# A linear-attention, gated-MLP and gated-convolution chain on one core: the left-over key block is padded to full height, the weight splits end in a one-pass sum, the list scheduler has other rules, and batch 2's attention is placed in batch 1

## The chip, the cores and the metric

The program runs on one core of one Trainium2 chip. A core has five engines that run their own instruction streams and wait for each other by semaphores: TensorE (PE, matmuls into PSUM), VectorE (DVE), ScalarE (ACT, activations and copies), GpSimd (POOL) and SyncE (SP, which here issues nearly all DMA transfers). The metric is the device time of one execution in microseconds (us), as the median over runs; lower is better.

## The reference, cut to what matters

Three blocks follow one another, with B = 8 batches, 8 heads of 64, 576 tokens, model width 512 and inner width 1024:

```python
# 1 attention without a score matrix (q, k, v: [8, 8, 576, 64])
q_s = softmax(q, over the 64 of a head);  k_s = softmax(k, over the 576 tokens)
x = q_s @ (k_s^T @ v)                      # heads are put side by side: [8, 576, 512]
# 2 spatially gated MLP
u, v = split(gelu_tanh(x @ w_in), 2)       # 512 wide each
v_n = layernorm(v) * g_ln
x2 = x + (u * (w_sg @ v_n + b_sg)) @ w_out
# 3 convolution gate
h = relu(x2 @ w_in2)                       # 1024 wide
c = depthwise_conv3(h, conv_w)             # along the tokens
out = (h * sigmoid(c)) @ w_out2
```

The weights arrive as 64-bit floats and have to be used at more than single-pass precision. So the kernel writes each operand as a high part and a low part, both in a 32-bit format that TensorE takes in one pass (`F32R`), and makes each product from three matmuls (hi·hi, hi·lo, lo·hi; `mm3`, L477).

## The kernel before

**Phases.** Phase 1 does blocks 1 and 2 for batches 0 to 7, phase 2 does block 3 for all batches. Block 2's result goes to a DRAM tensor `x2d` and is read back in phase 2. A batch of phase 1 is a list of 29 groups (L1186 on): four `hv` units (the v half of x @ w_in, 128 tokens each), eight `hu` units (the u half), eight `mx` units (w_sg times v_n), and eight `wo` units (times w_out). The function `insert(b, i)` (L1165) puts the attention of a later batch behind group `i` of batch `b`.

**Attention of a batch.** `attend_k` (from `k_steps`, L605) takes the maximum of the key tile `kt` over the tokens on DVE: maxima over column blocks (`top`), then transposes and swaps (`spread`), all in the scratch tiles `scr` and `r`; POOL subtracts it from `kt`, ACT takes the exponential. The keys lie as [128 tokens, 4 blocks of 512 columns], and the 64 tokens that are left over from 576 = 4·128 + 64 stand in a fifth, half-wide block of `kt`: its upper 64 partitions hold heads 0 to 3, its lower 64 the others. `attend_q` (`q_steps`, L665) does the softmax of the query tiles `q0` to `q3`, and the left-over query tile `q4` has its own seven steps (`left_max` to `left_tr` in `k_steps`, scratch `lm` and `lx`). `back_kv(b, c2)` (L707) multiplies the keys with the values `vt` for two of four pairs of heads; the ones column of `vt` gives the softmax sum, and DVE divides by it into `kvd`. For the left-over block its matmuls contract over 64 rows alone. It is called twice for a batch, and the second call issues the loads of the next batch's `kt` and `vt`. `xt` and `xt_left` multiply `kvd` with the queries.

**Weights.** `split` (L485) turns a 64-bit weight block into its two parts with bit operations on DVE and copies on ACT. For 12 blocks the low part is summed on TensorE (L522): `one`·a − hi + `one`·lf, where `one` is the identity matrix in F32; 32 further blocks of 256 columns (`split_far`) are summed on POOL and written to DRAM for phase 2.

**Order.** The code above issues nothing by itself. Each call is recorded, with a price (`price`, L220) and its dependences, and `Plan.order` (L285) simulates the engines: TensorE takes whole units (from `begin` to `begin`), the first one that would not stall among the next `WINDOW` = 8; the other engines take the ready instruction whose latest start is smallest. The sequence that comes out is what each engine's stream holds, so the recorded line of every instruction is L429, in `emit`. Two of the rules are touched: how long a DVE instruction and a POOL instruction that meet hold each other up (`start`, L327), and the choice of an instruction (L406 on).

Of the kernel before, what the change touches and what calls it, by code (L numbers as in the profile page):

```python
# [152 lines left out]
class Plan:  # L153
    WINDOW = 8
# [32 lines left out]
    def add(self, eng, name, args, kw):  # L187
        n = self.node(eng, name, args, kw)
        out = kw["out"] if "out" in kw else args[0]
        ins = [a for a in list(args[0 if "out" in kw else 1:]) + [v for k, v in kw.items() if k != "out"] if isinstance(a, View)]  # L190
        for v, w in [(a, False) for a in ins] + ([(out, True)] if isinstance(out, View) else []):
            self.touch(n, v, w)
        self.price(n, out, ins)
        return n
# [25 lines left out]
    def price(self, n, out, ins):  # L220
# [10 lines left out]
        elif e == "pe":  # L231
            m = size(out)
            if name == "transpose":
                n.cost = 0.22
            elif ins[0].tile.dtype == F32:
                n.cost = 0.09 if m == 65 else 0.71 if m == 512 else 0.19
            else:
                n.cost = max(0.111, 0.0045 + m * 0.000447)
            n.lat = n.cost + 0.17
        elif e == "act":  # L240
            n.cost = (0.155 if psum else 0.195) + cols * 0.00085
            if isinstance(n.kw.get("scale"), View) or isinstance(n.kw.get("bias"), View):
                n.cost += 0.05 + min(cols, 500) * 0.0001
            n.lat = n.cost + 0.07
            f = args_func(n)
            n.table = {"Gelu_apprx_tanh": "g", "Exp": "e", "Sigmoid": "s"}.get(f)
        elif e == "pool":
# [3 lines left out]
            if "tensor" in name:  # L251
                wide = any(o[0] == "to_broadcast" for v in views for o in v.ops)
                n.cost = 0.95 if cols == 1 else 0.2 + cols * (0.0008 if name == "tensor_copy" else 0.00164 if wide else 0.0021)
# [3 lines left out]
            n.shared = True  # L257
        else:
            two = sum(v.tile.space != "psum" for v in ins) > 1 and not psum and name in ("tensor_tensor", "scalar_tensor_tensor")
# [5 lines left out]
            n.shared = (two or fast) and cols > 60  # L265
# [19 lines left out]
    def order(self):  # L285
# [20 lines left out]
        poolend = [0.0]  # L306
        vecend = [0.0]
# [19 lines left out]
        def start(n, t):  # L327
# [3 lines left out]
            if n.eng == "dve" and n.shared and poolend[0] > t:  # L331
                more = min(cost, poolend[0] - t) * 1.0
                cost, lat = cost + more, lat + more
            if n.eng == "pool":
                if vecend[0] > t:
                    more = min(0.5, vecend[0] - t)
                    cost, lat = cost + more, lat + more
                poolend[0] = t + cost
            if n.eng == "dve" and n.shared:
                vecend[0] = t + cost  # L340
# [32 lines left out]
        while events:  # L373
# [4 lines left out]
            while again:  # L378
                again = False
                for k in self.real:  # L380
# [30 lines left out]
                    if can:  # L411
                        key = lambda n: (n.late + (2.0 if n.table and n.table != table[0] else 0.0), n.i)
                        n = min(can, key=key)
                        queue[k].remove(n)
                        start(n, t)
                        again = True
# [3 lines left out]
        return out  # L420

# [16 lines left out]
def attn_gated_conv_kernel(ctx, tc, q, k, v, q0, k0, w_in, g_ln, w_sgT, b_sg, w_out, w_in2, conv_w, w_out2, out):  # L438
# [46 lines left out]
    def split(slot, src, hi, lo, n, modes, stores=(), behind=None):  # L485
# [11 lines left out]
        lf, hf = l.bitcast(F32), h.bitcast(F32)  # L497
# [10 lines left out]
        dve.tensor_scalar(h, a.bitcast(U32), 0xFF800000, None, ALU.bitwise_and)  # L508
        (pool if hi is not None else dve).tensor_tensor(lf, lf, hf, ALU.mult)
        if hi is None:  # L510
            dve.tensor_tensor(lo, a, lf, ALU.add)
            return
        if modes is None:
# [6 lines left out]
            pe.matmul(ps, one, lf, start=False, stop=True)  # L520
            act.activation(lo, ps, AF.Copy)
            return  # L522
        modes[0].tensor_tensor(a, a, r32(hi), ALU.subtract)
        modes[1].tensor_tensor(lo, a, lf, ALU.add)
        for t, d in zip((hi, lo), stores):
            sp.dma_start(d, r32(t))
# [45 lines left out]
    vt = at.tile([128, 18, 2, 65], F32, name="vt")  # L572
    qt = {b: [None] * 5 for b in range(B)}
# [5 lines left out]
    def q_tile(b, c):  # L579
        qt[b][c] = at.tile([128, 512 if c < 4 else 256], F32, tag=f"q{c}", name=f"q{c}", bufs=2)  # L580
        return qt[b][c]

    def load_q(b):
        for c in range(4):
            sp.dma_start(q_tile(b, c), q[b, :, c * 512:c * 512 + 512])

    def load_left(b):
        sp.dma_start(q_tile(b, 4), q[b, :, 2048:2304])

    def load_v(b):  # L590
        sp.dma_start(vt[:, :, :, 0:64], v[b])
# [13 lines left out]
    def k_steps(b):  # L605
# [29 lines left out]
        def ex():  # L635
            act.activation(kt, kt, AF.Exp)

        qv = qt[b][4].rearrange("p (j a) -> p j a", a=32)
        lm = at.tile([128, 8], F32, tag="lm", name="lm")
        lx = at.tile([128, 8], F32, tag="lx", name="lx")  # L640

        def left_max():
            dve.tensor_reduce(lm, qv, axis=AX.X, op=ALU.max)
            swap32(lx, lm, CFG['sl'][min(b - 1, 2)])
            dve.tensor_tensor(lm, lm, lx, ALU.max)
            pool.tensor_tensor(qv, qv, lm.unsqueeze(2).to_broadcast([128, 8, 32]), ALU.subtract)

        def left_exp():
            act.activation(qv, qv, AF.Exp)
            dve.tensor_reduce(lm, qv, axis=AX.X, op=ALU.add)  # L650

        def left_mul():
            swap32(lx, lm, CFG['sl'][min(b - 1, 2)])
            dve.scalar_tensor_tensor(lm, lm, 1e-9, lx, ALU.add, ALU.add)
# [917 lines left out]
```

## Time and profile before

| | us |
|---|---|
| median of 3 runs | 951.65 |
| lowest and highest run | 951.44 and 953.36 |
| span of the profiled execution | 952.6 |
| TensorE busy, VectorE busy | 926.2, 772.9 |
| ScalarE busy, GpSimd busy | 543.7, 317.8 |

The profiled execution is told by its span, from its first instruction to its last; nothing that lies around the span is listed for it. Its span lies between the lowest and the highest run, 0.95 us above the median. A matmul's recorded duration is a modelled one and overlaps the next matmul's; how fast TensorE goes is read from the distance between two starts. Almost all rows carry L429, so groups are told apart by the names of their tiles: `mm` and `acc` are PSUM tiles, `wsl` the staging tile of the weight blocks for phase 2, `wAh` and `wAl` the parts of w_in. An F32 matmul has two records in the trace, an F32R matmul one.

### The profile page before, as it was taken

The page shows a single profiled execution, that of the slowest core. Times are in us where ns is not written, and L with a number is a line of the kernel's source. Part 1 is how long each engine was busy: PE and PEld are TensorE (multiplying, and loading weights), DVE is VectorE, ACT ScalarE, POOL GpSimd, SP SyncE. Part 2 cuts the span into 40 slices and gives each one's busy share as a digit, 9 for nine tenths or more (in the row PEclk, how much of TensorE's full clock was granted, in tenths as well). Part 3 has the DMA queues.
Part 4 walks back from the last instruction along what each step waited for, and adds up shares of the span by engine and source line. Part 5 has one row for each costly group of instructions (what it writes and reads, how often), then busy time and mean ns, then how long its engine had stood idle before and what let it go on. Part 6 is the DMA issues. An engine that isn't in the chain of part 4 may idle for free.

```text
span 952.6 us, 16062 instructions
## 1 busy us (share of the span) xinstructions
PE 926.2 (97%) x6026; PEld 821.1 (86%) x6026; DVE 772.9 (81%) x1477; ACT 543.7 (57%) x1113; POOL 317.8 (33%) x334
## 2 busy tenths in 40 slices
PE   5999999999999999999999999999999999999997
PEld 4578877988988889889899999998989888988895
DVE  7978989888888879889876348998798969886773
ACT  6776454655746645635643335544767656675663
POOL 6335454555636635737634000201120202020000
PEclk9999999999999999999999999999999999999999
DMA  9741614172482653812548572001111111121011
GB/s 316 194 147 32 175 65 116 43 201 69 119 208 78 193 133 94 215 59 90 122 138 256 154 218 71 34 12 70 37 50 45 73 34 51 45 73 34 7 39 56
DMA packets 54663, 99.17 MB, mean 104 GB/s; under 512 B 5332, under 2 KB 29012, under 8 KB 52792
## 3 DMA queue, kind: packets, MB, share of 16 engines
q1 hardware_dynamic: 50888, 89.88, 30.1%
q0 software_dynamic: 3696, 8.26, 5.0%
q8 instruction: 47, 0.77, 0.3%
q14 instruction: 32, 0.26, 0.1%
HBM read 62.59 MB, written 35.53 MB: 103 GB/s over the span
## 4 chain that ended last, share of the span: by engine, by line
PE 85%; DVE 9%; DMA 2%; ACT 2%; issue 1%; POOL 0%; SPq 0%; ACTq 0%
PE mm L429 57%; PE acc L429 28%; DVE wsl L429 2%; DVE sm L429 1%; DMA wsl<-in_w_in 1%; DVE scr L429 1%; DMA wsl<-in_w_out 1%; DVE r L429 1%; DVE vnl L429 1%; DVE xl L429 1%; DVE gl L429 1%; DMA sgh<-in_q 1%; DVE lm L429 0%; DVE u L429 0%; DVE x2s L429 0%
## 5 line engine op out<-in xcount | busy, mean ns | idle before, releaser
L429 DVE SCALAR_TENSOR_TENSOR cv<-h,cw,cv 128x576 f32<-128x576 f32 x128 | 111.9, 875 | 17.3 <-ACT cv L429 15.5
L429 PE MATMUL acc<-wAh,yl 128*128 128x512 f32 x256 | 101.8, 397 | 0.0
L429 PE MATMUL acc<-wAh,yh 128*128 128x512 f32 x256 | 100.8, 394 | 0.7 <-ACT yh L429 0.7
L429 PE MATMUL acc<-wAl,yh 128*128 128x512 f32 x256 | 101.0, 395 | 0.0
L429 PE MATMUL mm<-sgh,vnh 128*128 128x288 f32 x256 | 81.4, 318 | 1.5 <-DVE u L429 1.0
L429 PE MATMUL mm<-xh,w2h 128*128 128x288 f32 x280 | 82.8, 296 | 0.0
L429 PE MATMUL mm<-xh,w2l 128*128 128x288 f32 x280 | 82.4, 294 | 0.0
L429 PE MATMUL mm<-xl,w2h 128*128 128x288 f32 x280 | 82.4, 294 | 0.0
L429 PE MATMUL mm<-xh,wAh 128*128 128x288 f32 x256 | 79.3, 310 | 2.9 <-DVE xl L429 1.4
L429 PE MATMUL acc<-gh,wouth 128*128 128x288 f32 x256 | 81.2, 317 | 0.0
L429 PE MATMUL acc<-gl,wouth 128*128 128x288 f32 x256 | 76.3, 298 | 1.1 <-DVE gl L429 1.0
L429 PE MATMUL mm<-sgh,vnl 128*128 128x288 f32 x256 | 75.5, 295 | 0.6 <-DVE vnl L429 0.6
L429 PE MATMUL acc<-gh,woutl 128*128 128x288 f32 x256 | 75.8, 296 | 0.0
L429 PE MATMUL mm<-xh,wAl 128*128 128x288 f32 x256 | 75.5, 295 | 0.0
L429 PE MATMUL mm<-xl,wAh 128*128 128x288 f32 x256 | 75.5, 295 | 0.0
L429 PE MATMUL mm<-sgl,vnh 128*128 128x288 f32 x256 | 75.4, 294 | 0.0
L429 ACT ACTIVATE cv<-cv 128x576 f32<-128x576 f32 x64 | 43.7, 683 | 54.7 <-DVE cv L429 54.7
L429 POOL TENSOR_TENSOR wsl<-wsl 128x256 f32<-128x256 f32 (+1 forms) x66 | 50.7, 768 | 60.5 <-DVE wsl L429 23.7
L429 POOL TENSOR_TENSOR q<-q,qm 128x512 f32<-128x512 f32 x56 | 61.5, 1123 | 20.5 <-DVE qm L429 18.9
L429 POOL TENSOR_TENSOR kt<-kt,scr 128x512 f32<-128x512 f32 (+1 forms) x42 | 48.3, 1176 | 48.9 <-PE acc L429 23.3
L429 POOL TENSOR_TENSOR xf<-xf 128x576 f32<-128x576 f32 x12 | 21.0, 1751 | 128.4 <-DVE xl L429 99.4
L429 DVE TENSOR_TENSOR cv<-cv,h 128x576 f32<-128x576 f32 x64 | 52.2, 816 | 13.0 <-ACT cv L429 12.2
(281 smaller groups left out, 2913.9 us busy)
## 6 DMA issues: line engine op xcount, KB each, us to landing
x2d<-x2s SPq DMA_DIRECT2D x16, 576.0 KB, 4.3
kt<-in_k SPq DMA_DIRECT2D x7, 1152.0 KB, 5.3
vt<-in_v SPq DMA_DIRECT2D x7, 1152.0 KB, 10.0
x2d<-xl POOLq DMA_DIRECT2D x7, 1152.0 KB, 10.6
xf<-x2d SPq DMA_DIRECT2D x7, 1152.0 KB, 5.1
q<-in_q SPq DMA_DIRECT2D x28, 256.0 KB, 2.7
out<-ot SPq DMA_DIRECT2D x28, 256.0 KB, 2.0
wsl<-in_w_in SPq DMA_DIRECT2D x16, 256.0 KB, 3.7
```

The source lines that it names most:

```text
L429: getattr(self.real[n.eng], n.name)(*[val(a) for a in n.args], **{k: val(v) for k, v in n.kw.items()})
```

## The change

1. *Left-over block.* `vt` grows from 18 to 20 blocks: the left-over values stand once in the upper 64 partitions (for heads 0 to 3) and once in the lower 64, with zeros in the other half, so that every matmul of `back_kv` contracts over 128 rows. `back_kv` handles all four pairs of heads in one unit and one PSUM tile, with one set of divisions in place of two. The values come by three transfers in place of one.
2. *Queries.* The four tiles and the left-over tile become one tile [128, 4, 576]; the left-over's own steps go, and each of the four blocks has 576 columns in place of 512.
3. *Splits.* The third matmul of a sum is −1·lo with both operands in F32R, in place of `one`·lf in F32. A small value is caught by a maximum with `GUARD` on absolute values (ACT `Abs`, DVE `tensor_scalar` max) in place of a square on ACT and a compare-and-multiply on DVE.
4. *Scheduler.* `WINDOW` is 12; some prices differ; of a DVE and a POOL instruction that both use SBUF tensors in the named ways the later one starts when the earlier is done; ACT and DVE may wait for a more urgent instruction that is about to be ready (`pick`).
5. *Placement.* Batch 2's attention moves from groups 24 to 27 of batch 0 to groups 9 to 12 of batch 1, and its `xt` from group 8 on to group 14 on. The exponential of the keys is issued in three pieces.

```diff
-    WINDOW = 8
+    WINDOW = 12
@@ price, of a POOL instruction
-            n.shared = True
+            n.shared = "tensor" in name
@@ price, of a DVE instruction
-            n.shared = (two or fast) and cols > 60
+            n.shared = not psum and name in ("tensor_tensor", "scalar_tensor_tensor", "tensor_scalar", "tensor_copy")
@@ start
-            if n.eng == "dve" and n.shared and poolend[0] > t:
-                more = min(cost, poolend[0] - t) * 1.0
...
-            if n.eng == "pool":
-                if vecend[0] > t:
-                    more = min(0.5, vecend[0] - t)
...
+            if n.shared:
+                more = max(0.0, port[n.eng] - t - 0.12)
                 cost, lat = cost + more, lat + more
+                port["dve" if n.eng == "pool" else "pool"] = t + cost
@@ choice of an instruction
-                        n = min(can, key=key)
+                        n = self.pick(k, sorted(can, key=key), queue[k], t, table, first < len(units) and units[first][0].late)
+    def pick(self, k, can, waiting, t, table, now):
+        n = can[0]
+        if k not in self.HOLD or now is False or n.late - now < self.NEAR:
+            return n
+        for n in can:
...
+                       and m.late < n.late - 1.0 and m.late - now < self.NEAR for m in waiting):
+                return n
+        return None
@@ split
-        act.activation(lf, l, AF.Copy, scale=2.0 ** -52)
-        dve.tensor_scalar(a.bitcast(U32), h, 3, 0x3FFFFFF8, ALU.logical_shift_left, ALU.bitwise_and)
-        dve.scalar_tensor_tensor(a.bitcast(U32), h, 0xC0000000, a.bitcast(U32), ALU.bitwise_and, ALU.bitwise_or)
-        act.activation(hf, hf, AF.Square)
-        dve.scalar_tensor_tensor(a, hf, GUARD * GUARD, a, ALU.is_ge, ALU.mult)
+        act.activation(a, hf, AF.Abs)
+        act.activation(lo if summed else lf, l, AF.Copy, scale=-(2.0 ** -52) if summed else 2.0 ** -52)
+        dve.tensor_scalar(a, a, GUARD, None, ALU.max)
+        dve.tensor_scalar(au, au, 3, 0x3FFFFFF8, ALU.logical_shift_left, ALU.bitwise_and)
+        dve.scalar_tensor_tensor(au, h, 0xC0000000, au, ALU.bitwise_and, ALU.bitwise_or)
...
+            pool.tensor_tensor(lo, r32(lo), hf, ALU.mult)
...
-            pe.matmul(ps, one, lf, start=False, stop=True)
+            pe.matmul(ps, neg, lo, start=False, stop=True)
@@ load_v
-        sp.dma_start(vt[:, :, :, 0:64], v[b])
+        sp.dma_start(vt[:, 0:16, :, 0:64], v[b, :, 0:16])
+        for e in range(2):
+            r = slice(64 * e, 64 * e + 64)
+            sp.dma_start(vt[r, 16 + 2 * e:18 + 2 * e, :, 0:64], v[b, r, 16:18])
@@ back_kv
-                        r = slice(0, 64) if hp < 2 else slice(64, 128)
-                        pe.matmul(o, kt[r, c:c + 64], vt[r, 16 + i, e], start=False, stop=True)
+                    c = t * 512 + hp * 128 + 64 * e if t < 4 else 2048 + hp % 2 * 128 + 64 * e
+                    pe.matmul(o, kt[:, c:c + 64], vt[:, t * 4 + hp, e], start=(t == 0), stop=(t == 4), skip_group_check=True)
...
+            dve.tensor_tensor(kvd[r, :, r], pv[r, :, 0:64], rt[r].unsqueeze(2).to_broadcast([64, 4, 64]), ALU.mult)
@@ insert
+    XT = {b: (b - 1, 17 if b == 1 else 14 if b == 2 else 8 if b % 2 == 0 else 12) for b in range(1, B)}
+    KV = {b: (max(b - 2, 0), 26) for b in range(1, B)}
+    KV[1], KV[2] = (0, 15), (1, 11)
```

What the scheduler makes of it is seen in the engines' streams. First TensorE at the start, where batch 0's keys meet its values (`vt`, `kt`) and the first weight sums (`one`, `neg`) follow. Before:

```order
L429 MATMUL mm_179<-vt_85,kt_163 64x65 x20
L429 MATMUL mm_150<-one_80,sgh_98 128x128 x2
L429 MATMUL mm_189<-vt_85,kt_163 64x65 x20
L429 MATMUL mm_138<-q_1_225,kvd_91 128x512
...
L429 MATMUL mm_150<-vnh_133,one_80 128x512
L429 MATMUL mm_150<-wAh_315,neg_87 128x512
L429 MATMUL mm_150<-vnh_133,one_80 128x512
```

And after, in the same place:

```order
L441 MATMUL mm_178<-vt_85,kt_162 64x65 x40
L441 MATMUL mm_149<-one_80,sgh_96 128x128 x2
L441 MATMUL mm_188<-q_224,kvd_94 128x512
...
L441 MATMUL mm_137<-vnh_132,one_80 128x512
L441 MATMUL mm_137<-wAh_295,neg_87 128x512
L441 MATMUL mm_137<-wAl_271,neg_87 128x512
```

The two groups of 20 matmuls have become one of 40, and the last matmul of a sum has `neg` as its second operand in place of `one`.

Second VectorE at the end of batch 0's groups. `u` is the product that an `mx` unit of TensorE hands over, `gl` the low part that a `wo` unit waits for; `scr` and `r` are the key maximum of batch 2. Before:

```order
L429 TENSOR_TENSOR scr_147<-scr_147,kt_163 64x256 x2
L429 STREAM_TRANSPOSE scr_147<-scr_147 128x512
L429 TENSOR_REDUCE r_0_684<-scr_147 128x16
L429 COPY r_0_754<-r_0_684 64x16 x2
...
L429 STREAM_TRANSPOSE scr_147<-r_0_684 128x512
L429 TENSOR_TENSOR u_597<-mm_189,u_597 128x288
L429 TENSOR_TENSOR xl_0_1061<-mm_179,xh_0_1017 128x512
L429 TENSOR_TENSOR gl_786<-u_597,gh_757 128x288
L429 TENSOR_TENSOR xl_0_1061<-mm_138,xh_0_1017 128x512
L429 COPY lx_800<-lm_789 32x8 x2
L429 TENSOR_TENSOR lm_789<-lm_789,lx_800 128x8
L429 TENSOR_TENSOR u_681<-mm_150,u_681 128x288
```

After, the last three `u` of batch 0:

```order
L441 TENSOR_TENSOR u_584<-mm_149,u_584 128x288
L441 TENSOR_TENSOR scr_146<-kt_162 128x512
L441 TENSOR_TENSOR gl_770<-u_584,gh_766 128x288
...
L441 TENSOR_TENSOR u_675<-mm_188,u_675 128x288
L441 TENSOR_TENSOR scr_146<-scr_146,kt_162 128x512
L441 TENSOR_TENSOR gl_718<-u_675,gh_711 128x288
...
L441 TENSOR_TENSOR scr_146<-scr_146,kt_162 64x256 x2
L441 TENSOR_TENSOR u_117<-mm_137,u_117 128x288
L441 STREAM_TRANSPOSE scr_146<-scr_146 128x512
L441 TENSOR_TENSOR gl_770<-u_117,gh_766 128x288
L441 TENSOR_REDUCE r_0_688<-scr_146 128x16
```

The whole chain of `scr` and `r` stood in front of one `u`; now its pieces stand between the `u` and `gl`, and most of it behind the last of them; the instructions on `lm` and `lx` are gone.

Third the transfers that SP issues when the key and value tiles come free, here for batch 2. Before:

```order
L429 DMA x2s_155<-in_w_sgT 64x576 x2
L429 DMA xh_0_143<-in_w_out 128x1024 x2
L429 DMA kt_163<-in_k 128x2304
L429 DMA vt_85<-in_v 128x36x64
L429 DMA q_0_130<-in_q 128x256
```

And after:

```order
L441 DMA vt_85<-in_v 64x4x64
L441 DMA vt_85<-in_v 128x32x64
L441 DMA kt_162<-in_k 128x2304
L441 DMA vt_85<-in_v 64x4x64
L441 DMA q_120<-in_q 128x576 x2
```

The keys stood ahead of the values; for batches 2 to 7 they now stand behind the large part of them.

## Rows read from the trace of the kernel before

**Rows 1.** First part of the page: busy time, share, instructions.

```profile
PE 926.2 (97%) x6026; PEld 821.1 (86%) x6026; DVE 772.9 (81%) x1477; ACT 543.7 (57%) x1113; POOL 317.8 (33%) x334
```

**Rows 2.** Busy by stretch: length, PE, PEld, DVE, ACT, POOL, clock, DMA share, GB/s.

```profile
0.00:39.00 39.00, 27.31 (x153) 16.42 (x153) 30.86 (x59) 27.21 (x52) 21.76 (x35) 1.00 0.81 260
39.00:108.00 69.00, 69.00 (x425) 55.20 (x424) 59.49 (x121) 48.28 (x97) 31.63 (x30) 1.00 0.41 122
108.00:138.00 30.00, 26.63 (x215) 22.95 (x214) 26.52 (x63) 12.97 (x18) 16.25 (x18) 0.94 0.24 69
138.00:451.40 313.40, 307.49 (x2261) 278.03 (x2260) 275.72 (x584) 175.52 (x363) 170.64 (x185) 1.00 0.47 127
451.40:560.90 109.50, 109.50 (x726) 102.48 (x724) 69.51 (x155) 43.66 (x94) 35.70 (x43) 1.00 0.59 172
560.90:952.60 391.70, 386.28 (x2257) 346.00 (x2255) 310.82 (x500) 236.06 (x491) 41.81 (x25) 1.00 0.15 51
```

**Rows 3.** Chain of waits up to 129: start us, us, what.

```profile
20.07 13.34 PE mm L429 x108
...
38.42 43.54 PE mm L429 x198
...
117.50 0.71 DVE scr L429
...
124.38 4.62 PE mm L429 x12
```

**Rows 4.** Timeline of DVE and of POOL, 118 to 125: start us, us, what.

```profile
120.56 1.81 DVE L429 COPY lx<-lm 32x8 f32<-32x8 f32 x2
122.41 1.18 DVE L429 TENSOR_TENSOR lm<-lm,lx 128x8 f32<-128x8 f32 x1
...
118.34 6.71 POOL L429 TENSOR_TENSOR kt<-kt,scr 128x512 f32<-128x512 f32 x6 [6.05 <-PE mm L429]
```

**Rows 5.** Timeline of PE, 51.6 to 54: a weight sum.

```profile
51.67 0.39 PE L429 MATMUL mm<-wAh,xl 128*128 128x512 f32 x1
51.90 1.02 PE L429 MATMUL mm<-lt,one 128*128 128x512 f32 x2
52.35 0.80 PE L429 MATMUL mm<-wAh,neg 128*128 128x512 f32 x1
52.99 1.06 PE L429 MATMUL mm<-xl,one 128*128 128x512 f32 x2
53.89 0.40 PE L429 MATMUL mm<-x2s,one 128*128 128x288 f32 x1
```

**Rows 6.** Timeline of PE, batch 0's second key-value group; then one matmul's min/median/max ns.

```profile
23.06 0.69 PE L429 MATMUL mm<-vt,kt 128*64 128x65 f32 x16
...
23.68 0.95 PE L429 MATMUL mm<-vt,kt 64*64 64x65 f32 x20
...
24.82 4.54 PE L429 MATMUL mm<-q,kvd 128*128 128x512 f32 x16
...
L429 PE MATMUL mm<-vt,kt x640: 218/222/370, 20.0 to 446.8; 128*64 128x65 f32 x128, 64*64 64x65 f32 x32
```

**Rows 7.** DVE groups by form: busy us, mean ns, idle before.

```profile
L429 DVE TENSOR_REDUCE qm<-q 128x16 f32<-128x512 f32 x56 | 35.6, 674 | 1.4 <-ACT q L429 1.3
...
L429 DVE TENSOR_REDUCE lm<-q 128x8 f32<-128x256 f32 x14 | 5.6, 403 | 0.6 <-ACT q L429 0.5
...
L429 DVE SCALAR_TENSOR_TENSOR xl<-xh,xl 128x512 f32<-128x512 f32 x6 | 4.1, 687 | 3.6 <-ACT xh L429 3.5
...
L429 DVE RECIPROCAL lm<-lm 128x8 f32<-128x8 f32 x7 | 1.4, 203 | 0.2
...
L429 DVE TENSOR_SCALAR xh<-xl 128x512 uint32<-128x512 uint32 x6 | 2.6, 430 | 0.2
```

**Rows 8.** DMA issues: count, KB each, median us from issue to landing.

```profile
kt<-in_k SPq DMA_DIRECT2D x7, 1152.0 KB, 5.3
vt<-in_v SPq DMA_DIRECT2D x7, 1152.0 KB, 10.0
```

More of the change, by code (lines that the diff above doesn't have):

```diff
@@ L420, in order @@
         return out
+    NEAR = 6.0
+    def pick(self, k, can, waiting, t, table, now):
[3 more added lines that the diff above has]
+        for n in can:
+            end = t + n.cost + (1.28 if n.table and n.table != table[0] else 0.0)
+            swap = k == "act" and n.table and n.table != table[0]
+            if not any(t < m.ready < end + (1.28 if swap and m.table and m.table != n.table else 0.0) - 0.1
+                       and m.late < n.late - 1.0 and m.late - now < self.NEAR for m in waiting):
+                return n
+        return None
+    HOLD = ("act", "dve")
     def emit(self):
@@ L496, in split @@
             h, l = raw[:, :, 1], raw[:, :, 0]
-        lf, hf = l.bitcast(F32), h.bitcast(F32)
+        lf, hf, au = l.bitcast(F32), h.bitcast(F32), a.bitcast(U32)
+        summed = hi is not None and modes is None
         ld = sp.dma_start(raw, src)
@@ L571, in attn_gated_conv_kernel @@
     kt = at.tile([128, 2304], F32, name="kt")
-    vt = at.tile([128, 18, 2, 65], F32, name="vt")
-    qt = {b: [None] * 5 for b in range(B)}
+    vt = at.tile([128, 20, 2, 65], F32, name="vt")
+    qt = {}
     scr = at.tile([128, 512], F32, name="scr")
@@ L635, in ex, with red @@
         def ex():
[L636 to L654, printed above, removed]
-            dve.reciprocal(lm, lm)
-            pool.tensor_tensor(qv, qv, lm.unsqueeze(2).to_broadcast([128, 8, 32]), ALU.mult)
-        def left_tr():
-            t = qt[b][4]
-            dve.transpose(out=t, in_=t)
-        return [top, spread, sub, ex, left_max, left_exp, left_mul, left_tr,
-                ]
+            for i in range(3):
+                c = slice(i * 768, (i + 1) * 768)
+                act.activation(kt[:, c], kt[:, c], AF.Exp)
+        return [top, spread, sub, ex]
     def q_steps(b):
-        q3 = [t.rearrange("p (j a) -> p j a", a=32) for t in qt[b][0:4]]
-        qm = at.tile([128, 64], F32, tag="qm", name="qm")
-        qx = at.tile([128, 64], F32, tag="qx", name="qx")
+        q3 = [qt[b][:, c].rearrange("p (j a) -> p j a", a=32) for c in range(4)]
+        qm = at.tile([128, 72], F32, tag="qm", name="qm")
+        qx = at.tile([128, 72], F32, tag="qx", name="qx")
         def cols(c):
-            return slice(c * 16, c * 16 + 16)
-        def red(cs, op):
+            return slice(c * 18, c * 18 + 18)
+        def red(c, op):
             def go():
-                for c in cs:
-                    dve.tensor_reduce(qm[:, cols(c)], q3[c], axis=AX.X, op=op)
+                dve.tensor_reduce(qm[:, cols(c)], q3[c], axis=AX.X, op=op)
             return go
@@ L752, in xt @@
         ps = mm_tile()
-        pe.matmul(ps, kvd[:, hp], qt[b][hp], start=True, stop=True)
+        pe.matmul(ps, kvd[:, hp], qt[b][:, hp, 0:512], start=True, stop=True)
         act.activation(x_hi[b][:, hp, 0:512], ps, AF.Copy)
@@ L873, in attn_gated_conv_kernel @@
     pool.memset(nhalf, -0.5)
-    pool.memset(vt[:, :, :, 64:65], 1.0)
+    pool.memset(vt[:, 0:16, :, 64:65], 1.0)
+    pool.memset(vt[:, 16:20], 0.0)
+    for e in range(2):
+        pool.memset(vt[64 * e:64 * e + 64, 16 + 2 * e:18 + 2 * e, :, 64:65], 1.0)
     xL = {}
@@ L901, in attn_gated_conv_kernel @@
         sp.dma_start(q0t[:, qts[i]], q0[:, qts[i]])
-    vst = [(4 * c, at.tile([128, 512 if c < 4 else 256], F32, tag=f"q{c}", bufs=2)) for c in range(5)]
+    vst_ = at.tile([128, 4 * S], F32, tag="q", bufs=2)
+    vst = [(4 * c, vst_[:, 512 * c:min(512 * c + 512, 4 * S)]) for c in range(5)]
     for c, (g, t) in enumerate(vst):
@@ L921, in attn_gated_conv_kernel @@
         pool.memset(r32(lt2[e][o:o + 2]), 1.0)
-    sm = p1.tile([128, 96], F32, name="sm")
+    sm = wk.tile([128, HALF], F32, tag="u", name="u", bufs=4)
     nk, qmx, qsm = sm[:, 0:4], sm[:, 8:44], sm[:, 48:84]
@@ L1019, in attn_gated_conv_kernel @@
     load_q(1)
-    load_left(1)
     s_xl()
-    for c in range(2):
-        back_kv(0, c)
+    back_kv(0)
     for hp in range(4):
```

141 lines of the change are left out of this document (61 added, 80 removed).

## The prediction, made before the changed kernel was run

> **What bounds the kernel now.** I read the page's first part, then a table of stretches, the chain of waits, and last the timelines and groups of the places that the chain named. TensorE is busy for 926 of 952.6 us [rows 1], and in the stretches after 451 it is the bound almost alone: idle for nothing up to 560.9 and for 5.4 us in phase 2 [rows 2]. The reader is to see that time can be won in two ways only: less TensorE work in phase 1, or less of its idle time before 451. That idle time is 11.7 us in the first 39, none to 108, 3.4 from 108 to 138, and 5.9 from 138 to 451.4 (length less PE busy) [rows 2]. Its nearest rival is VectorE, at 86% from 39 to 108, 88% in each of the next two stretches, and lower after 451 (63%, then 79%) [rows 2].
>
> Two places stand out. At the start, TensorE's first part ends at 33.41, and its next unbroken piece begins at 38.42 [rows 3]: between them the chain runs through ACT, DVE and POOL, which prepare the third and fourth weight block. At the end of batch 0 the chain goes through DVE up to 124.38 [rows 3]: first the key maximum of batch 2 (`scr`), then three small instructions on `lx` and `lm` that take 1.81 and 1.18 us, while POOL works from 118.34 to 125.05 [rows 4]. A reciprocal on the same 128x8 tile takes 0.20 on average [rows 7]; here the small ones last as long as a POOL instruction does. The idle time also costs clock: the granted clock over 108 to 138 is 0.94 [rows 2], and the 12 matmuls from 124.38 take 4.62 us [rows 3], where 0.23 each, the distance of two starts in [rows 5], would make 2.8. That is 1.8 us at the lower of the two levels, 1.2 GHz, after the idle time.
>
> **The change, part by part.**
>
> *Sums.* An F32 pass lasts from 52.99 to 53.89, 0.90 us; a one-pass matmul of 512 columns 0.23 (51.67 to 51.90) [rows 5]. The third matmul of a sum turns from the one into the other: 0.67 less. There are 12; the first four stand before 39 and are counted with the start. Eight stand in the stretch to 108, where TensorE is never idle: 8 x 0.67 = 5.4 us. If a weight block came late it would be nothing.
>
> *Keys times values.* A pair of heads takes 0.88 (23.06 to 24.82 for two) [rows 6]: eight full-height matmuls start from 23.06 on, the two half-height ones from 23.68 on, so these take 0.26, 0.13 each. The eight full ones end 0.69 after the first start [rows 6]; less 0.22 for the last one itself that is seven steps in 0.47, 0.067 each, and the step right after the half-height ones is among them, so a steady step is at most that, perhaps 0.06. Ten full-height steps: 0.60 to 0.67, so 0.21 to 0.28 saved a pair, 0.84 to 1.12 a batch. For batches 1 to 7: 5.9 to 7.8 us; I take 7, nearer the steady step, because one unit also has one change of height less at either end. Batch 0's are counted with the start.
>
> The Trainium skill has a rule against this (TensorEngine Tiling (Array Packing), Performance Considerations, When to Use Tiling): a contraction of 64 rows is a case for two row tiles, up to twice as fast, and padding it to 128 gives that up. By it nothing would be saved here. The trace doesn't agree: 0.13 for a half-height matmul against 0.067 [rows 6]. The same page's Tiling Modes, Key Properties, says that a change of the mode drains TensorE, which would explain it: here the mode changes for two matmuls and back.
>
> *The start.* Four sums (2.7) and batch 0's keys (about 1) come off the work before 38.42, and DVE's chain to the third and fourth block gets shorter: per block one instruction of 0.687 becomes one of the 0.430 kind [rows 7]. But the end of that wait is the later of the two chains, and ACT now gets `Abs` in front of DVE's first instruction. Between 0 and the whole 5.0 I take 3.5. What of it doesn't come is hidden behind the two POOL products and DVE.
>
> *VectorE's load.* The six forms on `lm`, `lx` and the 256-column query tile go; the first and the last of them in busy time are 5.6 and 1.4 [rows 7], and all six add up to 21. The 64 columns come back in 56 reductions and 28 transposes: 674/512 x 64 = 84 ns [rows 7], for both forms, 7.1 us. A main weight block saves about 0.3 (a 0.687 for a 0.430, and a contiguous source), 12 x 0.3 = 4; the far blocks of 256 columns are taken as no gain; half as many divisions in the keys-times-values step, 16 small instructions fewer of 0.15 to 0.2, 3 at least. Together 21 - 7.1 + 4 + 3 = 21 us of VectorE, about 5% of its 393 us up to 451 [rows 2]. So VectorE shrinks more than TensorE's work (4%), and should not become the bound by itself. ACT and POOL (56% and 54% of 138 to 451 [rows 2]) lose small instructions too, and their terms are taken as nothing: VectorE and TensorE cover them.
>
> *The end of batch 0.* Batch 2's key maximum no longer stands ahead of an `u`, and `lx` and `lm` are gone. The price on the path was 3.4 idle and 1.8 of clock. I take 4.5 of the 5.2; none, if batch 1's own queries take that place on DVE.
>
> *Later stalls.* Of the 5.9 idle us from 138 to 451 some 70% should go with VectorE's load (4.2). Against that stands a new wait: batch 2's and batch 3's keys now both fall into batch 1, and batch 3's keys have to land (up to 10.0, since they stand behind the values [rows 8]), be maximised, be subtracted by POOL (6.7, [rows 4]) and exponentiated in the time of half a batch, about 30. What is queued behind that wait on DVE is an `u`, so TensorE would stand for it. I take 2 us. Net 2.2, between 5.9 and -5.
>
> *No price.* Phase 2 has the same work; its stalls stay. Loads of the queries move behind `xt_left(0)`; they are two batches ahead, hidden by TensorE's work. Two small value transfers more per batch are issued by SP, which waits on nobody there.
>
> Sum: 5.4 + 7 + 3.5 + 4.5 + 2.2 = 22.6, and 952.6 - 22.6 = 930.0 for the profiled execution. Nothing around its span is listed; it is 0.95 above the median of the runs, so the forecast is 929.
>
> **The rivals.**
>
> 1. *VectorE paces phase 1.* For it: 88% busy over 343 us, and instructions that wait for POOL. Against it: it loses more than TensorE does. Then the 12.4 us of sums and keys turn into waits, and 942.4, as a median 941.5, is left.
> 2. *The stall moves from batch 0 into batch 1.* For it: two attentions in one batch. Against: DVE's order puts the pieces of `scr` between the `u`. Then the 4.5 is not won and 5 come on top: 939.5, median 938.5.
> 3. *Slower: the keys wait behind the values.* From batch 2 on SP issues the large value transfer first. In the trace the keys, issued first, land after 5.3 and the values after 10.0 [rows 8]; turned about, the keys land up to 4.7 later, six times. If DVE, which works strictly in its order, stands at its first `scr` for all of it: 28 us, and 930 + 28 = 958, median 957. It is slower than before from 3.8 us a batch on (22.6 over six). Against it: the key chain of batches 3 to 7 had slack before, and a dozen DVE instructions stand between batch 2's division and batch 3's first `scr`; none of them needs the transfer.
> 4. *The padded block saves nothing*: 937, median 936. This is the time that follows if half-height matmuls are not the slow ones; the rows speak against it. The skill's rule on row tiles (the page and section above) would give this.
> 5. *Nearly all stalls go*, and some of the short waits that a modelled matmul end hides: the start 5.0, the clock and idle 5.2, the later 5.9, the keys 7.8, the sums 5.4, and about 3 hidden: 32, so 920, median 919.
>
> **How the numbers follow.** Forecast 0.54 (its own range 922 to 936), rival 1 0.13, rival 2 0.11, rival 3 0.06, rival 4 0.04, rival 5 0.10, and 0.02 that gains and losses cancel. A measurement of this kernel tells some 0.2% from no change, 1.9 us. Everything but rival 3 and the last 0.02 is faster: 0.92 faster, 0.02 the same, 0.06 slower. The range from 915 to 943 takes in rivals 1, 2, 4 and 5 and leaves out rival 3 and the extremes.
>
> **What would show it.** In the changed kernel's profile: a sum of some 1.33 us on TensorE in place of 1.99; a keys-times-values group of 40 matmuls of 2.4 to 2.8 us; no `lx` and `lm`; no granted clock below 1.00 near the end of batch 0; phase 2's first matmul near 538 in place of 561, and phase 2 itself 391 to 392 long. The forecast is wrong if VectorE's share up to that point rises over 92% while TensorE's idle time grows (rival 1), if `scr` waits for the transfer of the keys for over 3 us a batch (rival 3), or if TensorE idles where batch 3's keys meet its values (rival 2).

## The result, and the profile after

The changed kernel takes 928.6 us (median of 4 runs, 927.97 to 928.96); the kernel before took 952.5 in the same comparison. The ratio is 0.9745, with a 95% interval from 0.9723 to 0.9768. The forecast was 929.0.

First part of the page of the changed kernel (busy us, share, instructions), which answers to [rows 1]:

```profile
PE 904.2 (98%) x6014; PEld 813.6 (88%) x6014; DVE 737.4 (80%) x1395; ACT 536.5 (58%) x1074; POOL 315.1 (34%) x324
```

TensorE is busy 22.0 us less and VectorE 35.5 us less, in a span that is 25.7 us shorter (926.9).

The next two fences are the view of [rows 2] (stretch, its length, busy us of PE, PEld, DVE, ACT, POOL, granted clock, DMA share, GB/s), cut where the work is cut: at the first matmul of batch 0 and at the first of phase 2. First the kernel before, whose start and phase 2 are in [rows 2]:

```profile
39.00:560.77 521.77, 512.49 (x3621) 458.54 (x3619) 431.11 (x920) 280.43 (x570) 254.22 (x274) 1.00 0.47 133
```

Then the changed kernel:

```profile
0.00:35.79 35.79, 22.87 (x149) 15.59 (x149) 26.67 (x53) 25.56 (x49) 22.52 (x39) 1.00 0.74 259
35.79:536.05 500.26, 495.20 (x3612) 451.91 (x3610) 401.49 (x844) 273.44 (x534) 248.87 (x261) 1.00 0.50 140
536.05:926.90 390.85, 386.14 (x2258) 346.13 (x2256) 309.27 (x500) 237.48 (x491) 43.75 (x25) 1.00 0.15 51
108.00:138.00 30.00, 30.00 (x178) 26.71 (x177) 25.33 (x57) 16.41 (x24) 14.06 (x14) 1.00 0.12 35
```

The 25.7 us come in four pieces: the start, 39.00 less 35.79, 3.2; TensorE's busy time in phase 1, 512.49 less 495.20, 17.3; its idle time there, 9.28 less 5.06, 4.2; and phase 2, 391.83 less 390.85, 1.0. The last row is the end of batch 0: busy for all of its 30.00 us at a granted clock of 1.00, where [rows 2] had 26.63 and 0.94.

PE's timeline of the changed kernel (start us, us, what): a weight sum and the start of the next, and one batch's keys times values. They answer to [rows 5] and [rows 6].

```profile
63.34 1.02 PE L441 MATMUL mm<-xl,one 128*128 128x512 f32 x2
63.79 0.80 PE L441 MATMUL mm<-wAh,neg 128*128 128x512 f32 x1
64.43 0.39 PE L441 MATMUL mm<-wAl,neg 128*128 128x512 f32 x1
64.66 1.02 PE L441 MATMUL mm<-xl,one 128*128 128x512 f32 x2
...
236.67 2.55 PE L441 MATMUL mm<-vt,kt 128*64 128x65 f32 x80
239.15 0.40 PE L441 MATMUL acc<-gh,wouth 128*128 128x288 f32 x1
```

A sum now takes 1.32 us from start to start (63.34 to 64.66), where it took 1.99 (51.90 to 53.89). The 40 matmuls of a batch take 2.48 (236.67 to 239.15), where two groups of 1.76 (23.06 to 24.82 in [rows 6]) made 3.52.

DMA issues of the changed kernel (KB each, median us from issue to landing), which answer to [rows 8], and below them SP's queue in batch 1 (start us, us):

```profile
kt<-in_k SPq DMA_DIRECT2D x7, 1152.0 KB, 10.0
vt<-in_v SPq DMA_DIRECT2D x7, 1024.0 KB, 7.5
...
144.03 1.70 SPq L441 DMA_DIRECT2D vt<-in_v  x2
145.83 4.40 SPq L441 DMA_DIRECT2D kt<-in_k  x1
```

The keys land 4.7 us later than before, as the third rival had it. No wait of TensorE or VectorE on `kt`'s transfer shows.

### The profile page after: what moved, and what is told of

Its sections match the earlier page's. It is cut to its first block, busy times and chain, and to the rows that moved or that the text cites. A ratio compares the mean times of both kernels' runs of the same rounds, so it can differ in the third digit from the quotient of the medians.

```text
span 926.9 us, 15888 instructions
## 1 busy us (share of the span) xinstructions
PE 904.2 (98%) x6014; PEld 813.6 (88%) x6014; DVE 737.4 (80%) x1395; ACT 536.5 (58%) x1074; POOL 315.1 (34%) x324
## 4 chain that ended last, share of the span: by engine, by line
PE 88%; DVE 4%; ACT 2%; DMA 1%; POOL 1%; issue 1%; POOLq 0%; ACTq 0%
PE mm L441 58%; PE acc L441 30%; DMA wsl<-in_w_in 1%; DVE xl L441 1%; DMA wsl<-in_w_out 1%; DVE scr L441 1%; DVE vnl L441 0%; POOL rd L441 0%; ACT L441 0%; DVE st L441 0%; POOL q L441 0%; POOL wsl L441 0%; DVE wsl L441 0%; DVE v L441 0%; DVE gl L441 0%
## 5 line engine op out<-in xcount | busy, mean ns | idle before, releaser
L441 POOL TENSOR_TENSOR q<-q,qm 128x576 f32<-128x576 f32 x56 | 66.3, 1214 | 23.8 <-DVE qm L441 18.0
L441 POOL TENSOR_TENSOR wsl<-wsl 128x256 f32<-128x256 f32 x64 | 46.2, 721 | 49.9 <-DVE wsl L441 17.8
L441 ACT ACTIVATE gh<-u 128x288 fp32r<-128x288 f32 x64 | 28.3, 443 | 59.2 <-DVE u L441 59.0
L441 DVE TENSOR_TENSOR yl<-cv,yh 128x512 fp32r<-128x512 f32 x64 | 48.7, 761 | 17.0 <-ACT yh L441 16.3
```

The lines of the kernel that those rows point to most:

```text
L441: getattr(self.real[n.eng], n.name)(*[val(a) for a in n.args], **{k: val(v) for k, v in n.kw.items()})
```

## The experiments

All ratios are to the kernel before on the same chip, with 95% intervals; it took 952.6 us beside e1 to e4, 952.1 beside e5 to e8 and 952.0 beside e9 to e12. "Busy" and "idle" in the table are TensorE's in phase 1, read as in the two fences of stretches above. The spans of the profiled executions lie up to 3.7 us under the medians of their kernels (and 0.1 and 0.3 above for the kernel before and e10), so kernels are compared by medians, and places within them by profiles.

"Clock" is TensorE's granted clock over a whole execution, the lowest and the highest of the runs. Over some 930 us, 0.001 of it is at most 0.9 us (an estimate from these two numbers). The changed kernel and e8 have 0.999 or more in every execution, e3 to e7 and e9 to e11 in none. So where an idle stretch is told below, the medians pay for idle time and for lowered clock together, and "busy" holds the second.

| run | median us | ratio (interval) | busy | idle | clock |
|---|---|---|---|---|---|
| before | 952.5 | 1 | 512.5 | 9.3 | 0.995 to 1.000 |
| e1 changed, again | 928.7 | 0.9744 (0.9725 to 0.9763) | 495.2 | 5.3 | 0.999 to 1.000 |
| e2 F32 third pass | 938.8 | 0.9852 (0.9832 to 0.9872) | 501.6 | 6.4 | 0.997 to 1.000 |
| e3 two groups, half height | 944.6 | 0.9917 (0.9892 to 0.9942) | 506.6 | 8.1 | 0.994 to 0.998 |
| e4 two groups, full height | 937.4 | 0.9835 (0.9811 to 0.9860) | 497.3 | 8.9 | 0.996 to 0.997 |
| e5 attention 2 in batch 0 | 935.1 | 0.9816 (0.9794 to 0.9838) | 497.8 | 8.3 | 0.994 to 0.996 |
| e6 old planner rules | 938.2 | 0.9847 (0.9824 to 0.9869) | 497.8 | 10.0 | 0.995 to 0.998 |
| e7 new planner alone | 956.2 | 1.0035 (1.0021 to 1.0049) | 512.9 | 11.3 | 0.995 to 0.998 |
| e8 keys issued first | 928.4 | 0.9743 (0.9722 to 0.9765) | 495.0 | 3.3 | 0.999 to 1.000 |
| e9 padded block alone | 954.6 | 1.0024 (1.0010 to 1.0037) | 506.9 | 15.9 | 0.995 to 0.997 |
| e10 padded block and sums | 948.7 | 0.9953 (0.9935 to 0.9972) | 503.1 | 15.8 | 0.993 to 0.998 |
| e11 no holding back | 933.5 | 0.9791 (0.9770 to 0.9812) | 497.9 | 6.0 | 0.995 to 0.998 |
| e12 move alone | 953.0 | 1.0003 (0.9988 to 1.0017) | 511.4 | 8.8 | 0.995 to 1.000 |

**e1.** The changed kernel unaltered. Expected:

> The changed kernel unaltered, on the same chip as the three that follow, as the mark to measure them from. Every theory expects the time already seen, 928.6 us, within 0.2%: 927 to 930.5.

Measured: 928.72. It is the mark for e2 to e6, e8 and e11.

**e2.** The third pass in F32 again, otherwise the changed kernel.

```diff
-            pool.tensor_tensor(lo, r32(lo), hf, ALU.mult)
+            pool.tensor_tensor(lf, lf, hf, ALU.mult)
...
-            pe.matmul(ps, neg, lo, start=False, stop=True)
+            pe.matmul(ps, one, lf, start=False, stop=True)
```

Expected:

> The changed kernel with one part undone: the third matmul of each weight sum is again a full F32 pass over `lf` (0.90 us in place of 0.23), with its price in the planner left as it is, so that every engine keeps its order and VectorE its work. Theory A (TensorE is the bound of phase 1, its removed work is the gain): 8 sums behind 36 us by 0.66 are 5.3 us, so 934; up to 936.5 if the four at the start count too. Theory B (VectorE's lighter load is the gain, and TensorE's removed work would only turn into waiting): no change, 928 to 930.

Measured: 938.8, 10.1 more than e1, and above theory A's 936.5. TensorE's busy time in phase 1 rose by 6.4 where 8 sums are 5.3, idle time by 1.1, and batch 0 began 1 us later. Theory B (no change) falls: the work that was put back doesn't fill idle time, and VectorE's busy time there is the same, 401.6 against 401.5. The size is more than the work, and one premise of the expectation failed: the engines did not keep their order. In the two traces VectorE, ScalarE, GpSimd and SP have their instructions in different orders from batch 0 on, and ScalarE loads 37 function tables in place of 33. So the 10.1 is the pass and a new order together, and only the 5.3 is told by the work.

**e3 and e4.** Two groups of 20 matmuls; e3 has the left-over block at half height, e4 at full height.

```diff
-    for hp in range(4):                  # one PSUM tile, one division
+    for c2 in (0, 2):                    # a PSUM tile and a division each
+        for hp in (c2, c2 + 1):
...
-   pe.matmul(o, kt[:, c:c + 64], vt[:, t * 4 + hp, e], ...)
+   r = slice(0, 128) if t < 4 else slice(0, 64) if hp < 2 else slice(64, 128)   # e3; e4: all 128
+   pe.matmul(o, kt[r, c:c + 64], vt[r, t * 4 + hp, e], ...)
```

Expected of e3:

> The changed kernel with the keys-times-values step in two groups of 20 matmuls, one for each half of the left-over rows, and the 8 matmuls a batch on the left-over block at half height (64 rows) again. Theory A: against the next kernel, which differs in the height alone, 1.04 us a batch (3.5 less 2.48), 7 batches behind the start: 7.3 us more; with one more group of small VectorE instructions hidden, 936 to 937. Theory B, and also the view that a half-height matmul is no slower than a full one: equal to the next kernel within 1 us.

Expected of e4:

> The changed kernel with the keys-times-values step in the same two groups of 20 matmuls, but all of them at the full height of 128 rows against the zero-padded values. Its instructions stand in the same order as those of the kernel ahead of it on all engines; only the height of 8 matmuls a batch is another. Theory A: TensorE's work is that of the changed kernel, so 928.6 to 930. Theory B: VectorE has about 4 small instructions of 0.2 a batch more, some 0.8 us a batch, so 929 to 935, and the kernel ahead of it takes the same.

Measured: e3 less e4 is 7.2 us, where theory A had 7.3. The difference is clear of noise, but the runs of each of the two lie 4 to 8 us apart, so the match to 0.1 is chance. PE's timeline of e3, one batch's keys times values:

```profile
250.84 3.58 PE L441 MATMUL mm<-vt,kt 128*64 128x65 f32 x80
254.35 0.40 PE L441 MATMUL acc<-gh,wouth 128*128 128x288 f32 x1
```

The same place of e4:

```profile
243.85 2.55 PE L441 MATMUL mm<-vt,kt 128*64 128x65 f32 x80
246.34 0.40 PE L441 MATMUL acc<-gh,wouth 128*128 128x288 f32 x1
```

3.51 against 2.49, with the same order on all engines: the 8 half-height matmuls of a batch cost 1.02 us more than full-height ones, 7.1 over seven batches. The Trainium skill's rule (TensorEngine Tiling (Array Packing), Performance Considerations, When to Use Tiling), by which a contraction of 64 rows is a case for row tiles, is not tested by this: the gain there is that of two row tiles at work together, and here the half-height matmuls of a group all stand in the same 64 rows. What the runs show is that a few half-height matmuls among full-height ones are the slower choice.

The surprise is e4 against e1: 8.7 us for a second group, where theory A had up to 1.4. Timelines of DVE, POOL and PE of e4:

```profile
175.88 4.87 DVE L441 TENSOR_SCALAR wsl<-wsl 128x256 uint32<-128x256 uint32 x1
...
185.68 0.81 DVE L441 TENSOR_SCALAR wsl<-wsl 128x256 uint32<-128x256 uint32 x3
...
176.10 4.50 POOL L441 TENSOR_TENSOR q<-q,qm 128x576 f32<-128x576 f32 x4
...
182.11 0.40 PE L441 MATMUL acc<-gl,wouth 128*128 128x288 f32 x1 [3.07 <-DVE gl L441]
```

An instruction of VectorE that takes 0.27 us a little later (0.81 for three) takes 4.87 while POOL makes four query products, and TensorE stands 3.07 us for the `gl` behind it. The new order had put the two together. It is TensorE's longest wait in phase 1, whose idle time grew by 3.6; the other pieces of the 8.7 (2.1 of busy time, lowered clock in every execution, a start 0.8 later) were not followed one by one. The Trainium skill (SBUF — State Buffer, SBUF: two separate sides) calls the port that VectorE and GpSimd share an exclusive lock, held for a whole instruction. The trace agrees as far as it goes: VectorE's instruction lasts until 180.75, just past the end of the fourth product (180.60), and did not come to its end between two of them.

**e5.** Batch 2's attention back in batch 0.

```diff
-    KV[1], KV[2] = (0, 15), (1, 11)
+    KV[1] = (0, 15)
```

(and `XT[2]` back at step 8). Expected:

> The changed kernel with batch 2's attention back in batch 0 (keys times values at step 26 of batch 0, query products from step 8 of batch 1). Theory A (TensorE's removed work is most of the gain, the move only clears the end of batch 0): what comes back is at most the 3.4 us idle and 1.8 us of clock there, so 930 to 934. Theory C (the gain of 11.4 us in batch 1 is due to the move): 938 to 941. If VectorE's lighter load alone cleared the end of batch 0: 928 to 930.

Measured: 935.1, 6.4 more than e1: a little over theory A, well under theory C. The end of batch 0 in e5, first as a stretch, then as timelines of DVE, POOL and PE:

```profile
108.00:125.00 17.00, 12.06 (x122) 10.72 (x121) 15.23 (x34) 7.73 (x11) 11.22 (x10) 0.80 0.17 49
```

```profile
111.99 0.71 DVE L441 STREAM_TRANSPOSE scr<-r 128x512 f32<-128x512 f32 x1
112.63 0.65 DVE L441 TENSOR_TENSOR xl<-mm,xh 128x512 fp32r<-128x512 f32 x1
...
112.84 6.49 POOL L441 TENSOR_TENSOR kt<-kt,scr 128x512 f32<-128x512 f32 x6 [6.90 <-issue]
...
113.33 0.61 PE L441 MATMUL mm<-sgh,vnh 128*128 128x288 f32 x1 [2.27 <-DVE xl L441]
120.26 3.60 PE L441 MATMUL mm<-vt,kt 128*64 128x65 f32 x68 [2.42 <-ACT kt L441]
```

Idle time of 2.27 and 2.42, a granted clock of 0.80 over 17 us: TensorE waits first for an `xl` that VectorE reached late, behind batch 2's key maximum (`scr`, `r`), then for `exp(kt)`, which waits for POOL. A stall stands at the place of [rows 3, 4] again although `lx` and `lm` are gone; in the changed kernel it is the move, with the order that it brings, that keeps this place clear.

**e6.** The changed work in the old planner's order (window 8, old prices, no exclusive meetings, no holding back). The edit puts back the old `price` and `order`. Expected:

> The changed kernel's work and placement, ordered by the old planner (window of 8, old prices, the old share of the meetings of VectorE and GpSimd, no holding back). Theory A: TensorE's work is that of the changed kernel, some 8 us of idle time at most come back, so 929 to 937. Theory C (the order that avoids the meetings is the main gain): 940 or more, with several more microseconds of VectorE instructions drawn out beside GpSimd.

Measured: 938.2, 9.5 more than e1, beyond theory A by 1.2. ScalarE's groups differ (count, busy us, mean ns); of e6 first:

```profile
L430 ACT ACT_TABLE_LOAD x47 | 60.3, 1283 | 4.2 <-PE mm L430 2.2 <-PEq L1533 0.7 <-DVE vnl L430 0.4
```

of the changed kernel:

```profile
L441 ACT ACT_TABLE_LOAD x33 | 42.3, 1283 | 1.6 <-PEq L1544 0.7 <-PE mm L441 0.2
```

14 loads of function tables more, 18 us of ScalarE. That the time goes to these loads is not shown: the kernel before has 31 of them and takes 952.

**e7.** The new planner on the old work. Expected:

> The kernel before with the new planner's rules alone: window of 12, new prices, exclusive meetings, holding back. No TensorE work is removed and nothing is moved by hand. Theory A: only idle time can go, 11.1 us of it behind 39 us with the lost clock, so 945 to 954. Theory C: 940 or less.

Measured: 956.2, 0.35% slower than before, and outside both expectations. It has 33 table loads, hardly more than the 31 of before. DVE's timeline of e7 shows the old stall, somewhat longer (with `lm` 3.5 us in place of the 3.0 of [rows 4]):

```profile
122.73 3.37 DVE L440 COPY lx<-lm 32x8 f32<-32x8 f32 x4
```

So the planner's rules are worth 9.5 us with the new work and cost 4 with the old. Of the 4, the two profiled executions show only 0.8 (spans of 953.4 and 952.6); the kernel before lost clock in its profiled one, but not in most of the others (see the account of the prediction), and e7 has 0.995 to 0.998 in all 12.

**e8.** Keys ahead of values on SP.

```diff
+            ld.deps[kload[b].i] = "start"      # each value transfer behind its batch's keys
```

Expected:

> The changed kernel with the key transfer of batches 2 to 7 issued ahead of the value transfers, as before; in the changed kernel the keys land after 10.0 us in place of 5.3. Theory A (the keys have slack): the keys land about 4.7 us earlier and the time stays within 1.5 us of 928.7. If the keys' wait is paid in part (the third rival of the prediction, in small): up to 6 x 0.8 = 5 us less, 924 to 926.

Measured: 928.4, within 0.3 of e1. DMA issues of e8:

```profile
kt<-in_k SPq DMA_DIRECT2D x7, 1152.0 KB, 5.2
vt<-in_v SPq DMA_DIRECT2D x7, 1024.0 KB, 9.1
```

The keys land 4.8 us earlier, and the time is the same: they had slack. This is the nearest to a version that beats both kernels, and it doesn't.

**e9 and e10.** On the kernel before: the padded block alone, then with the new `split`.

```diff
-    vt = at.tile([128, 18, 2, 65], F32, name="vt")
+    vt = at.tile([128, 20, 2, 65], F32, name="vt")
...
-                        pe.matmul(o, kt[r, c:c + 64], vt[r, 16 + i, e], start=False, stop=True)
+                    pe.matmul(o, kt[:, c:c + 64], vt[:, t * 4 + hp, e], start=(t == 0), stop=(t == 4))
```

Expected of e9:

> The kernel before with the padded left-over block alone: values tile of 20 chunks, all 40 matmuls of a batch at full height, still two groups, old planner, old placement, old sums (and `sm` in another buffer, for room). Theory A (TensorE's removed work arrives in the time by itself): 8 batches by 1.04 are 8.3 us of TensorE work, 944 to 945. Theory D (what an edit does to the planner's order weighs as much as the work it removes, since each kernel is ordered anew): TensorE's busy time falls by 8 us, and the time by anything between 2 and 14 us, 938 to 950.

Expected of e10:

> The kernel ahead of this one with the one-pass sums of the changed kernel as well (the whole new `split`), old planner and placement. Theory A: another 8 x 0.66 = 5.3 us, up to 8 with the four sums at the start: 936 to 940. Theory D: TensorE's busy time falls by 8 us more, the time by something else: 932 to 946.

Measured: 954.6 and 948.7. The first is 0.24% slower than before, outside theory A and beyond even theory D. The stretch of e9's phase 1:

```profile
37.08:559.88 522.80, 506.89 (x3621) 455.34 (x3619) 430.01 (x921) 276.26 (x567) 253.86 (x274) 1.00 0.48 133
```

TensorE is busy 5.6 us less than before and idle 6.6 us more (15.9): what was removed came back as waiting. The span of e9 is even 0.8 shorter than the one profiled before (951.8 and 952.6). That its median is 2.6 longer fits the clock: all 12 executions of e9 have 0.995 to 0.997, with a median of 0.996, where 15 of the 25 of the kernel before beside them have 0.999 or 1.000, and 0.003 of 950 us is 2.9 (an estimate). Where it waits at the end of batch 0, from e9's timelines of DVE, POOL and PE:

```profile
118.58 2.42 DVE L429 COPY lx<-lm 32x8 f32<-32x8 f32 x2
121.03 1.18 DVE L429 TENSOR_TENSOR lm<-lm,lx 128x8 f32<-128x8 f32 x1
122.13 0.81 DVE L429 TENSOR_TENSOR u<-mm,u 128x288 f32<-128x288 f32 x2
...
117.16 6.52 POOL L429 TENSOR_TENSOR kt<-kt,scr 128x512 f32<-128x512 f32 x6 [6.79 <-DVE scr L429]
...
122.99 0.50 PE L429 MATMUL mm<-wAh,xh 128*128 128x512 f32 x1 [3.85 <-DVE u L429]
```

The same three small instructions beside the same POOL products as in [rows 4], and 3.85 us of TensorE for the `u` behind them. The waits of e10 are waits for VectorE too, 7.0 us in all on DVE's `kvd` and 5.7 on its `u`:

```profile
PE mm L429 <- DVE kvd L429: 7.0, 5, 2.3
PE mm L429 <- DVE u L429: 5.7, 3, 2.9
```

(view of waits over 39 to 560: us in all, times, the longest). In e10's profile the granted clock is 0.89 from 95 to 110 and 0.77 from 375 to 390, around the `kvd` waits of 1.05 (before 99.69) and 2.29 (before 380.75). In the changed kernel one wait for `u` of 1.8 is left, and none for `kvd`.

**e11.** The changed kernel's planner without holding back.

```diff
-    HOLD = ("act", "dve")
+    HOLD = ()
```

Expected:

> The changed kernel with the planner's holding back on ScalarE and VectorE taken out (an empty list of engines), exclusive meetings and prices kept. The old planner's rules cost 9.5 us here and had 47 loads of ScalarE's function tables in place of 33. If these loads are what the order is worth, and holding back is what saves them: several loads more than 33 and 932 to 938. If it is the prices and the exclusive meetings: about 33 loads and 928 to 931.

Measured: 933.5, 4.8 more than e1, with 39 table loads. So about half of e6's 9.5 goes with the holding back; the rest is the prices and the exclusive meetings together, which weren't tried apart. The number is the one that the table loads were to give, but the loads are not what the trace shows. TensorE's longest wait in e11 is for ScalarE's `vnh`, and ahead of `vnh` ScalarE stands 5.18 us for a weight transfer. Timelines of ACT and PE:

```profile
264.99 0.43 ACT L441 ACTIVATE wsl<-wsl 128x256 f32<-128x256 f32 x1 [5.18 <-DMA wsl<-in_w_in]
265.32 0.70 ACT L441 ACTIVATE vnh<-v,rd 128x512 fp32r<-128x512 f32 x1
...
266.08 0.40 PE L441 MATMUL mm<-sgh,vnh 128*128 128x288 f32 x1 [3.10 <-ACT vnh L441]
```

The granted clock from 260 to 275 is 0.89, and 0.89 again from 130 to 145, around its next longest wait (2.07): together 3.3 us of clock (15 x 0.11, twice).

**e12.** On the kernel before: batch 2's attention at the new place, nothing else.

```diff
+    KV[1], KV[2] = (0, 15), (1, 11)
```

Expected:

> The kernel before with batch 2's attention moved from batch 0 into batch 1, at the places of the changed kernel, and nothing else. Theory A: of the 3.4 us idle and 1.8 us of clock at the end of batch 0 most go, 947 to 950. Theory that the stall only moves into batch 1 where VectorE is as full (the prediction's second rival): 951 to 957. If the 11.4 us that the changed kernel won in batch 1 are due to the move alone: 938 to 942.

Measured: 953.0, no change. Timelines of DVE, POOL and PE of e12:

```profile
122.19 2.32 DVE L429 COPY lx<-lm 32x8 f32<-32x8 f32 x2
124.54 1.20 DVE L429 TENSOR_TENSOR lm<-lm,lx 128x8 f32<-128x8 f32 x1
...
121.95 5.90 POOL L429 TENSOR_TENSOR kt<-kt,scr 128x512 f32<-128x512 f32 x5 [10.24 <-issue]
...
127.31 0.41 PE L429 MATMUL acc<-gl,wouth 128*128 128x288 f32 x1 [1.88 <-DVE gl L429]
149.71 1.83 PE L429 MATMUL mm<-vt,kt 128*64 128x65 f32 x40 [1.55 <-issue]
```

`lx` and `lm` of batch 2 still meet POOL's products on its keys, now where batch 1 begins, and a second stall of 1.55 stands in batch 1. That is the prediction's second rival, in the kernel where the small instructions are still there.

## Why the prediction was right, point by point

| term | forecast | measured in the changed kernel |
|---|---|---|
| start | 3.5 | 3.2 (39.00 to 35.79) |
| sums | 5.4 | 8 x 0.67 = 5.4 (1.99 to 1.32) |
| keys times values | 7 | 7 x 1.04 = 7.3 (3.52 to 2.48) |
| end of batch 0 | 4.5 | 5.2: 3.4 idle and 1.8 of clock gone, against the profiled execution of the kernel before |
| later stalls | 2.2 | 0.8: all idle time fell by 4.2, of which 3.4 are in the row above |
| not forecast | 0 | 3.8: 2.8 of TensorE's busy time (17.3 less 5.4, 7.3 and 1.8) and 1.0 of phase 2 |
| sum | 22.6 | 25.7 |

The mechanism held, and so did the signs asked for: the sum at 1.32, the group at 2.48, no `lx` and `lm`, no lowered clock at the end of batch 0, phase 2 from 536.05. That 929 was met to 0.4 is luck: two things of size were off, and they nearly cancel. Between the profiled executions 3.1 us more went than forecast. And the forecast put the median 0.95 under the profiled time, where it came out 1.7 above.

The second comes from the execution that was profiled. On record are 53 executions of the kernel before with time and span: the time is 1.73 to 1.84 above the span in each, and some 2.0 in the changed kernel. So the profiled execution, with its span of 952.6, took some 954.4 (an estimate from these numbers), 2 above the median. Its granted clock is 0.997. Of the 53, the 31 with 0.999 or 1.000 took 950.27 to 952.78, the other 22, with 0.995 to 0.998, 952.93 to 956.98. Most executions of the kernel before thus do not pay the 1.8 of clock that the forecast counted at the end of batch 0; between medians 23.9 us went, and not 25.7.

The 2.8 of busy time that no removed work answers to stay open. Matmuls that are the same in both kernels took less: the 512 on `vnh` are busy for 109.5 us before and 107.9 after, the 512 on `gh` for 117.3 and 116.0, so steps between starts were drawn out there; short waits would do this, but none is shown. One reading of the prediction was off too: sixteen small instructions of 0.15 to 0.2 are 2.4 to 3.2, not 3 at least, which its 21 for VectorE hardly feels.

What the prediction did not see is how little its terms are worth one by one. It added 12.4 us of TensorE work as if it fell out of the time wherever it was taken. On the kernel before, the padded block alone gained nothing (e9), and with the sums 3.3 us (e10), because TensorE then waits for VectorE and runs at a lowered clock behind the waits: its first rival, which is false of the whole (VectorE at 401.5 of 500.3 us, TensorE idle for 5.1) and true of these parts. The sentence that carries the forecast is therefore, as argued here, the one on VectorE's load: 21 us less were forecast up to 451, 29.6 less are measured up to phase 2 (431.11 to 401.49).

And the planner got no term at all, among the edits without a price or elsewhere. With the new work its rules are worth 9.5 us (e6), about half of them by holding back (e11); with the old work they cost 4 (e7). Added up in one order, old planner first: sums and padding 3.3 (952.0 to 948.7, e10), then query layout, one group and the move 10.5 (948.7 to 938.2, e6), then the planner 9.5. In another order the shares would differ: the move is worth nothing alone (e12) and 6.4 as the last part (e5). The parts undone singly cost 10.1, 6.4 and 9.5, and the group 8.7 and 7.2: 41.9 in all, more than the whole gain of 23.9. In the traces waits that one part clears are open again when another is missing (e5, e9, e12), clock is lost behind them, and each edit is ordered anew, with meetings such as e4's. Only e3 against e4 is a part by itself.

The rivals: the second (the stall moves) is false of the whole, as batch 1 (from its first matmul to that of batch 2) went from 74.8 to 63.4, and TensorE is idle there for 0.3 (busy 63.09 of 63.40, from 116.1 to 179.5); it is what e12 shows. The third (keys behind values) had its landing time right, 10.0, and its price wrong: nothing (e8). The fourth (padding saves nothing) fell by e3 and e4. Of the fifth, idle time of 5.1 was left.

Open: the query layout, which takes away `lx` and `lm`, was not undone by itself. That it is what lets the removed TensorE work arrive is argued from the same stall in the kernel before, e7, e9 and e12, all with `lx`, and not shown by a run of its own. Nor were the new steps of the splits on ScalarE and VectorE, or the exponential in three pieces.

## What to carry to other kernels

Work taken from the engine that is busy 97% of the time pays only where its feeder has room: look at what stands in the feeder's queue ahead of the next operand, and give the feeder its relief in the same change. A list-scheduled kernel can't be judged by undoing one edit, since every edit makes a new order; compare edits that keep the order on all engines (e3 and e4), see in the traces whether they did (e2 was to and didn't), and take the others as effects of edit and order together. Look at the granted clock of every execution before a profile is taken for the median one. A small VectorE instruction beside long ones of GpSimd can cost the long ones' time, so look for such pairs first.

## What the runs showed of the hardware that was not expected

- A VectorE instruction of 0.27 us took 4.87, through four GpSimd instructions in a row (e4).
- SP's issue of the keys takes 4.40 us behind the value transfers (145.83), and the keys land after 10.0; issued first, they land after 5.2 (e8).
- Executions of one kernel differ in their granted clock, and the time follows it: 31 of 53 of the kernel before have 0.999 or 1.000 and took up to 952.78, the others 0.995 to 0.998 and from 952.93 on.
- Eight half-height matmuls among full-height ones cost 1.02 us a batch more than at full height, in the same order (e3, e4).
